# Softmax over two lanes a partition instead of four, and another order of work, in a dynamic convolution with a gated output

## The chip, the core and the metric

The kernel runs on one core of one Trainium2 chip. The metric is the time of the program on the device, in microseconds (us); lower is better. A core has five engines with queues of their own that run in order: TensorE (PE, with its weight loads PEld), VectorE (DVE), ScalarE (ACT), GpSimd (POOL) and SyncE (SP). SP only issues DMAs here, POOL and ACT issue some too. Engines meet through semaphores.

## What is computed

`x` is (8 lanes, 4224 positions, 192 channels), `weight_gen` is (8, 4224, 8 heads, 7 taps). First each position and head gets a softmax over its 7 taps, and the channels of a head (24 each) are convolved causally with these weights:

```
w = softmax(weight_gen, axis=-1)                 # max, subtract, exp, sum, divide
y[b,s,h,:] = sum_k w[b,s,h,k] * x_pad[b, s+k, h, :]
gate = sigmoid(sum_k conv_w[k] * y_pad[:, s+k, :])   # 5 taps, one weight a channel
out  = (gate * (y @ w_val)) @ w_out
```

All of it is in float32.

## The kernel before, in words

**Tiling.** The 4224 positions are cut into 36 groups: 88 positions, then 34 of 120, then 56. Groups go through the engines in pairs (`Pair`): pair 0 is the first group alone, pairs 1 to 17 have two groups, pair 18 is the last alone. A *stage* q is the stretch in which PE does the first step of pair q, the value product of pair q-1 and the output product of pair q-2.

**First step, a matmul with a band.** For a group, `xt` holds 126 positions of `x` on partitions. `tb` holds a band matrix: row i has, for each lane and head, the softmax weights at the places of the outputs that position i feeds. `bank` (L333) multiplies them into PSUM (256 small matmuls a pair), `evac` (L348) copies PSUM to `ringA`, `ringB` and `S` on ACT, `move` (L356, L358) fills holes in the rings by DMAs from POOL.

**How the band is made.** `Softmax` treats a *part* of about 500 positions at a time: `load` (weights of `weight_gen` into `wt`), `max`, `sub`, `exp`, `sum`, `recip`, `norm`, then `halo` (a DMA that copies the first 6 rows of the next block behind each partition's rows), `spread` (four copies on ACT that put the weights into `zt`, with zeros between them) and `store` (DMA of `zt` into `z` in DRAM). `clear_z` writes the zeros of `z` that no store covers. `load_t` (L307) then reads `z` with a pitch that is one half cell short of a row, so that row i lands shifted by i: that is the band. It takes 9 DMAs a group. Ten parts (`parts`, called s0, s1, s2 and p3 to p9 here) use two `z` in turn, and two `wt`.

**In `before`** a partition of `wt` holds 8 positions (`RM`) of four lanes (`LH`); even partitions hold lanes 0 to 3, odd ones lanes 4 to 7, so that `load` and `store` are two DMAs each.

**The rest.** `tap0` (ACT) and `tap` (DVE, L378) do the 5-tap convolution, `sigm` (ACT, L383) the sigmoid, `wvm_`, `wva_`, `wvd_`, `wvb_` (PE, L402 to L415) the value product, `gv` (DVE, L422, L425) multiplies both, `omA`, `omB` (PE, L433, L442) do the output product, `oev` (ACT, L448) evacuates it to `ot`, `store` of `Pair` (SP, L456) writes it out. The four output products of a pair use the PSUM banks ps3, ps3, ps1, ps2, so the second waits until `oev` of the first has emptied ps3.

**What sets the order.** Every step is put in a list by `at(time, step)`, or `st(offset, step)` from the stage's nominal time `when(q)`; at the end the list is sorted by time and issued. The times only order the instructions of each engine's queue: nothing on the chip waits for them. A part first used in pair q (q = 4, 6, ... 16 for p3 to p9) has its steps placed relative to stages q-4 to q-2. A stage with a `spread` in it is called a *spread stage* below (in `before`, stages 4, 6, ... 14, and stage 3 for p3); the stage after it is a *plain stage*.

**The weights** `w_val` and `w_out` arrive as 64-bit patterns and are converted by `convert_weights` (L133 to L144, 8 steps each for three column ranges), then placed by `place_weights` on ACT.

Of the kernel before, what the change touches and what calls it, by code (L numbers as in the profile page):

```python
# [16 lines left out]
def tile_dynconv_gated_moe(  # L17
# [23 lines left out]
    L = B  # L41
# [11 lines left out]
    W = LH * H  # L53
    CELL = 2 * W + 4
# [9 lines left out]
    RM = 8  # L64
# [102 lines left out]
    ROWS = HD * RM  # L167
    zb = [dpool.tile([(1 + 2 * ROWS) * PITCH], FP32, name=f"z{i}") for i in range(2)]

    def clear_z(i, lo, hi, eng):  # L170

        t, n = zb[i], (hi - lo) // P
        for u in range(2):
            dst = bass.AP(tensor=t.tensor, offset=t.offset + (1 + ROWS * u + lo) * PITCH,
                          ap=[[n * PITCH, P], [PITCH, n], [1, PITCH]])
            src = bass.AP(tensor=zero.tensor, offset=zero.offset, ap=[[zero.ap[0][0], P], [0, n], [1, PITCH]])
            eng.dma_start(out=dst, in_=src)
        if lo == 0:
            eng.dma_start(out=t[0:PITCH].rearrange("(p c) -> p c", p=14),
                          in_=zero[0:14, 0:PITCH // 14])  # L180

    class Softmax:


# [59 lines left out]
        def spread(self, e, o):
            R, n = self.R, self.n
            m = NPR - o
            w0, z0 = self.wt[:, 0, e + o, 0:1], zt[:, e, 0:1]
            to = HC2 * (1 - e) + ((e, 1) if e == 0 else (1, CELL))[o]
            src = bass.AP(tensor=w0.tensor, offset=w0.offset + K - 1 - o,
                          ap=[[w0.ap[0][0], self.np], [2 * ROW, R // 2], [2 * (ROW - 1), m], [n * ROW, LH], [K, H]])  # L250
            dst = bass.AP(tensor=z0.tensor, offset=z0.offset + to,
                          ap=[[z0.ap[0][0], self.np], [2 * DATA, R // 2], [CELL, m], [2 * H, LH], [2, H]])
            nc.scalar.copy(out=dst, in_=src)  # L253

        def store(self, engs):
            t, R = zb[self.zi], self.R
            for u in range(2):
                z = zt[u:u + 1]
                src = bass.AP(tensor=z.tensor, offset=z.offset, ap=[[2 * z.ap[0][0], self.np // 2], [DATA, R], [1, DATA]])
                dst = bass.AP(tensor=t.tensor, offset=t.offset + (1 + ROWS * u) * PITCH,  # L260
                              ap=[[R * PITCH, self.np // 2], [PITCH, R], [1, DATA]])
                engs[u % len(engs)].dma_start(out=dst, in_=src)

    class Group:
# [29 lines left out]
        def load_t(self, p, w, lo, hi, eng):  # L294
# [5 lines left out]
            off = (1 + self.s - PAD + lo - p.r0) * PITCH + HC2 + skip * CELL - HC2 * i0  # L300
            src = bass.AP(tensor=b.tensor, offset=b.offset + off,
                          ap=[[PITCH - HC2, hi - lo], [ROWS * PITCH, 2], [1, cells * CELL]])
# [3 lines left out]
                          ap=[[NW * d.ap[0][0], hi - lo], [CELLS * CELL, 2], [1, cells * CELL]])  # L306
            eng.dma_start(out=dst, in_=src)  # L307

    class Pair:
# [12 lines left out]
        def bank(self, gi, kind, b):  # L322
# [357 lines left out]
```

## Time and profile before

| | |
|---|---|
| median of 3 runs | 611.3 us (610.46 to 615.15) |
| the profiled execution | 613.28 us, span 611.5 us |
| mean granted TensorE clock | 0.888 |
| PE busy | 465.6 us (76%) |
| DVE busy | 408.8 us (67%) |
| ACT busy | 310.1 us (51%) |
| POOL busy | 309.9 us (51%) |
| DMA moved | 116.5 MB, mean 191 GB/s |

The span is what the profile covers of the 613.28 us. The chain that ended last is 34% PE, 19% DMA, 15% SP's queue, 13% "issue" (the engine waited for nothing that the profile shows), 8% POOL and 6% DVE. An engine's idle time counts only where another engine, or the end, waits for it.

### The profile page before, as it was taken

Reading aid. Unit: us, or ns where it says so; the run is one execution under the profiler, and the core shown is the slowest. Engines: PE = TensorE matmul, PEld = TensorE weight load, DVE = VectorE, ACT = ScalarE, POOL = GpSimd, SP = SyncE. Lnnn points to the kernel's source line nnn. Section 1 sums busy time; section 2 is a strip of 40 time slices with the busy share of each in tenths; the row PEclk is TensorE's granted clock in tenths of the full one; section 3 lists DMA queues with packets and bytes.
Section 4 is the critical chain, followed back from the end, with each engine's and each line's share of the span. In section 5 each row is a group of like instructions: output and inputs, shape, how many; then the busy total and the mean of one; then the engine's idle time right before and its main releaser. Section 6 shows DMA issues by size and latency. Waiting matters only on the chain.

```text
span 611.5 us, 15672 instructions
## 1 busy us (share of the span) xinstructions
PE 465.6 (76%) x6450; PEld 352.0 (58%) x6450; DVE 408.8 (67%) x311; ACT 310.1 (51%) x427; POOL 309.9 (51%) x532
## 2 busy tenths in 40 slices
PE   5030164768875998699968977996899599899996
PEld 3030153555754776468556846683767396686765
DVE  6708607479872979397849885796679584665950
ACT  5014165436634763675367537655564545545442
POOL 8362627554546184537634581647184709337400
PEclk9556587797988999799979997998899789999999
DMA  8775567573769676967794778678866957563334
GB/s 229 241 190 183 151 205 212 137 241 85 211 181 250 211 199 184 260 181 223 165 308 131 241 186 257 163 218 193 277 158 204 246 155 193 156 197 82 98 98 119
DMA packets 77005, 116.50 MB, mean 191 GB/s; under 512 B 20149, under 2 KB 58624, under 8 KB 76934
## 3 DMA queue, kind: packets, MB, share of 16 engines
q1 hardware_dynamic: 54650, 80.36, 44.3%
q0 software_dynamic: 21296, 34.46, 22.4%
q8 instruction: 51, 0.84, 0.6%
q10 hardware_dynamic: 988, 0.68, 0.4%
q14 instruction: 20, 0.16, 0.1%
HBM read 59.35 MB, written 43.53 MB: 168 GB/s over the span
## 4 chain that ended last, share of the span: by engine, by line
PE 34%; DMA 19%; SPq 15%; issue 13%; POOL 8%; DVE 6%; ACT 4%; POOLq 0%; ACTq 0%; DVEq 0%
SPq L307 12%; PE ps L333 11%; PE ps L433 8%; DMA wt<-in_weight_gen_dram 5%; PE ps L442 5%; PE ps L407 4%; DMA z<-zt 4%; POOL xt L276 3%; POOL ringA L356 3%; DVE aA L378 3%; DMA xt<-in_x_dram 3%; DMA wt<-wt 2%; PE ps L402 2%; PE ps L410 2%; PE ps L415 2%
## 5 line engine op out<-in xcount | busy, mean ns | idle before, releaser
L333 PE MATMUL ps<-tb,xt 126*32 126x120 f32 (+2 forms) x4608 | 142.2, 282 | 98.0 <-DMA tb<-z 40.1
L333 PEld LDWEIGHTS ps<-tb,xt 126*32 126x32 f32 x4608 | 132.6, 115 | 108.1 <-issue 78.9
L276 POOL DMA_DIRECT2D xt<-in_x_dram x264 | 157.2, 623 | 25.8 <-DMA ringA<-S 7.0
L378 DVE SCALAR_TENSOR_TENSOR aA<-ringA,wf,aA 128x1920 f32<-128x1920 f32 (+2 forms) x76 | 157.3, 2070 | 7.8 <-ACT aA L374 3.4
L358 POOL DMA_DIRECT2D ringB<-S x76 | 42.2, 560 | 223.4 <-ACT ringB L348 184.4
L433 PE MATMUL ps<-wf,aA 128*120 128x192 f32 (+2 forms) x576 | 110.5, 348 | 0.0
L433 PEld LDWEIGHTS ps<-wf,aA 128*120 128x120 f32 (+2 forms) x576 | 102.0, 200 | 13.6 <-issue 13.2
L422 DVE TENSOR_TENSOR aA<-ps,aA 128x960 f32<-128x960 f32 (+2 forms) x36 | 39.3, 1130 | 101.3 <-ACT ot L448 57.1
L448 ACT COPY ot<-ps 120x768 f32<-120x768 f32 (+2 forms) x72 | 55.7, 798 | 85.0 <-PE ps L442 53.1
L442 PE MATMUL ps<-wf,aB 64*120 64x192 f32 (+2 forms) x576 | 65.0, 356 | 37.6 <-ACT ot L448 37.6
L378 DVE SCALAR_TENSOR_TENSOR aB<-ringB,wf,aB 128x960 f32<-128x960 f32 (+2 forms) x76 | 86.9, 1144 | 2.0
L356 POOL DMA_DIRECT2D ringA<-S x152 | 81.8, 545 | 7.0 <-issue 4.2
L442 PEld LDWEIGHTS ps<-wf,aB 64*120 64x120 f32 (+2 forms) x576 | 48.7, 193 | 56.7 <-ACT ot L448 46.4
L407 PE MATMUL ps<-ringA,wva 128*128 128x480 f32 (+2 forms) x144 | 63.0, 581 | 3.5 <-ACT ringB L348 3.5
L253 ACT COPY zt<-wt 128x512 f32<-128x512 f32 (+5 forms) x40 | 34.2, 924 | 54.1 <-DMA wt<-wt 33.0
L208 DVE TENSOR_REDUCE mx<-wt 128x256 f32<-128x1792 f32 (+2 forms) x10 | 18.3, 1826 | 49.1 <-DMA wt<-in_weight_gen_dram 49.1
L348 ACT COPY ringA<-ps 128x480 f32<-128x480 f32 (+2 forms) x72 | 36.2, 556 | 27.3 <-PE ps L333 27.3
L407 PEld LDWEIGHTS ps<-ringA,wva 128*128 128x128 f32 x144 | 26.3, 193 | 40.0 <-issue 22.5
L374 ACT ACTIVATE aA<-ringA,wf 128x960 f32<-128x960 f32 (+2 forms) x38 | 37.5, 1031 | 14.5 <-DMA ringA<-S 14.5
L348 ACT COPY S<-ps 128x480 f32<-128x480 f32 (+2 forms) x36 | 19.9, 552 | 46.2 <-PE ps L333 46.1
L383 ACT ACTIVATE aA<-aA 128x1920 f32<-128x1920 f32 (+2 forms) x19 | 32.1, 1690 | 14.3 <-DVE aA L378 14.2
L425 DVE TENSOR_TENSOR aB<-ps,aB 128x480 f32<-128x480 f32 (+2 forms) x36 | 21.5, 637 | 20.8 <-ACT aB L383 20.8
(59 smaller groups left out, 383.0 us busy)
## 6 DMA issues: line engine op xcount, KB each, us to landing
xt<-in_x_dram POOLq DMA_DIRECT2D x264, 94.5 KB, 4.0
out_dram<-ot SPq DMA_DIRECT2D x68, 360.0 KB
tb<-z SPq DMA_DIRECT2D x239, 74.4 KB
z<-zt SPq DMA_DIRECT2D x16, 612.0 KB
wt<-in_weight_gen_dram SPq DMA_DIRECT2D x16, 448.0 KB
wt<-wt SPq DMA_DIRECT2D x9, 588.0 KB
z<-zero SPq DMA_DIRECT2D x4, 1071.0 KB
ringA<-S POOLq DMA_DIRECT2D x136, 30.0 KB, 2.8
```

The costliest lines, as they stand in the source:

```text
L276: eng.dma_start(out=self.xb[0:G * NW, j, 0:D], in_=src)
L307: eng.dma_start(out=dst, in_=src)
L333: nc.tensor.matmul(out=pa[Q * c:Q * c + Q, n * l:n * l + n], lhsT=g.xb[0:k, LH * u + l, C * h:C * h + Q], rhs=t[:, u, PAD // 2:(PAD + n) / ...
L348: nc.scalar.copy(out=dst, in_=pa)
L356: nc.gpsimd.dma_start(out=ringA[q:q + h, LH * u:LH * u + LH, p0:p0 + n], in_=St[p:p + h, :, 0:n])
L358: nc.gpsimd.dma_start(out=ringB[HD * u + q:HD * u + q + h, :, p0:p0 + n], in_=St[p:p + h, :, 0:n])
L378: nc.vector.scalar_tensor_tensor(out=a, in0=self.src(g, j), scalar=cw[:, g, j:j + 1], in1=a, op0=ALU.mult, op1=ALU.add)
L407: nc.tensor.matmul(out=self.v01(e)[:, u], lhsT=wva, rhs=self.A(e, u), start=True, stop=False)
L422: nc.vector.tensor_tensor(out=a, in0=self.v01(e), in1=a, op=ALU.mult)
L433: nc.tensor.matmul(out=ps[b][0:n, u, D * t:D * t + D], lhsT=g[:, u, t], rhs=woa, start=first and t == 0, stop=not first, skip_group_check= ...
L442: nc.tensor.matmul(out=ps[b][0:n, u, D * t:D * t + D], lhsT=g[hs, t], rhs=wob[hs], start=first and t == 0, stop=not first, skip_group_chec ...
L448: nc.scalar.copy(out=ots[0:n, 2 * e + k], in_=ps[b][0:n, :, 0:2 * D])
```

## The change

A partition of `wt` now holds 16 positions of two lanes (`LQ`), and partition 4b+u holds block b of lanes 2u and 2u+1. A cell of the band is half as wide, `tb` has four lane groups instead of two, and `load`, `store` and `clear_z` are four DMAs each. The bytes of `load` and `store` for a part are the same; the halo copies 6 rows of two lanes instead of four. The first part stores whole rows of `z`, zeros included, so nothing has to be cleared for it. Loads, `exp`, `halo`, the taps' sigmoids and much of the first 60 us have other places.

```
-    W = LH * H
-    CELL = 2 * W + 4
+    LQ = 2
+    NL = L // LQ
+    NBL = P // NL
+    W = LQ * H
+    CELL = 2 * W + 2
...
-    RM = 8
+    RM = 16
...
+            self.row = PITCH if i == 0 else DATA
+            self.z = zt[:, 0:R * self.row].rearrange("p (r c) -> p r c", r=R)
...
-                d, n = 2 * (c // R + 1), min(R, PAD - c)
+                d, n = NL * (c // R + 1), min(R, PAD - c)
...
-            for u in range(2):
-                z = zt[u:u + 1]
-                src = bass.AP(tensor=z.tensor, offset=z.offset, ap=[[2 * z.ap[0][0], self.np // 2], [DATA, R], [1, DATA]])
...
+            for u in range(NL):
+                z = self.z[u:u + 1]
+                src = bass.AP(tensor=z.tensor, offset=z.offset, ap=[[NL * z.ap[0][0], p], [self.row, R], [1, self.row]])
...
-                          ap=[[PITCH - HC2, hi - lo], [ROWS * PITCH, 2], [1, cells * CELL]])
+                          ap=[[PITCH - HC2, hi - lo], [ROWS * PITCH, NL], [1, cells * CELL]])
...
-                        rhs=t[:, u, PAD // 2:(PAD + n) // 2, l, h, :],
+                        rhs=t[:, (LH * u + l) // LQ, PAD // 2:(PAD + n) // 2, l % LQ, h, :],
...
-    at(7.1, s0.halo, (nc.sync, nc.scalar, nc.sync))
+    at(7.5, s0.halo, (A, A))
...
-    at(8.5, s1.exp)
+    at(11.55, s1.exp)
...
-            at(when(a) + (8.0 if q > 4 else 2.0), p.load, u, nc.sync)
+            at(when(q - 5) + 12.5 if q > 5 else when(1) + (1.0 if q < 5 else 12.0), p.load, u, SP)
...
+        at(t1 + 1.5 if q <= 4 else when(q - 3) + 7.5, p.exp)
...
-        at(when(a + 2) + 4.0, p.halo, (nc.sync,))
+        at(when(q - 2) + 3.3, p.halo, (SP,))
...
-            at(when(a + 2) + 8.0 + 0.9 * i, p.spread, i // 2, i % 2)
+            at(when(q - 2) + 8.0 + 0.01 * i, p.spread, i // 2, i % 2)
...
-            st(6.5, p1.sigm, 0)
-            st(11.0, p1.sigm, 1)
+            st(11.5 if q > 1 else 6.1, p1.sigm, 0)
+            st(16.4 if q > 1 else 6.5, p1.sigm, 1)
```

The tables of times move the following. In the rows a line number is that of the program, a name with a number is one buffer, "x4" means four in a row.

ACT in a spread stage and the end of it, before (L348 `evac`, L383 `sigm`, L253 `spread`, L363 the rings' halo, L448 `oev`, L374 `tap0`):

```order
L348 COPY ringA<-ps_92 128x4x120 x2
L383 ACTIVATE aA_76<-aA_76 128x1920
L253 COPY zt<-wt_65 128x4x4x32
L253 COPY zt<-wt_65 128x4x3x32
L253 COPY zt<-wt_65 128x4x4x32
L253 COPY zt<-wt_65 128x4x3x32
L383 ACTIVATE aB_79<-aB_79 128x960
L363 COPY ringA<-ringA 128x8x4
L363 COPY ringB<-ringB 128x4x4
L448 COPY ot<-ps_94 120x768
L374 ACTIVATE aA_77<-ringA,wf 128x960 x2
L448 COPY ot<-ps_94 120x768
```

and in the changed kernel:

```order
L354 COPY ringA<-ps_92 128x4x120 x2
L257 COPY zt<-wt_65 128x8x4x16
L257 COPY zt<-wt_65 128x8x3x16
L257 COPY zt<-wt_65 128x8x4x16
L257 COPY zt<-wt_65 128x8x3x16
L389 ACTIVATE aA_76<-aA_76 128x1920
L369 COPY ringA<-ringA 128x8x4
L369 COPY ringB<-ringB 128x4x4
L454 COPY ot<-ps_94 120x768
L380 ACTIVATE aA_77<-ringA,wf 128x960
L389 ACTIVATE aB_79<-aB_79 128x960
L380 ACTIVATE aA_77<-ringA,wf 128x960
```

The first `oev` stands ahead of the second sigmoid, which stood ahead of it, and the `spread` ahead of the first. The `exp` of the next part, which followed in before at the end of this stage (L216, with a table load), has gone to the plain stage, behind the evacuations there.

SP in a spread stage, before (L307 `load_t`, L234 `halo`, L199 `load`, L262 `store` of z, L456 output):

```order
L456 DMA out_dram<-ot 120x2x384 x4
L307 DMA tb_63<-z_97 14x2x476
L307 DMA tb_63<-z_97 14x2x680 x7
L307 DMA tb_63<-z_97 14x2x476
L234 DMA wt_66<-wt_66 112x4x336
L234 DMA wt_66<-wt_66 14x4x336
L307 DMA tb_64<-z_97 14x2x476
L307 DMA tb_64<-z_97 14x2x680 x7
L307 DMA tb_64<-z_97 14x2x476
L199 DMA wt_65<-in_weight_gen_dram 64x4x448 x2
L262 DMA z_98<-zt 512x1x306 x2
L456 DMA out_dram<-ot 120x2x384 x4
```

and in the changed kernel:

```order
L202 DMA wt_65<-in_weight_gen_dram 32x2x896 x4
L462 DMA out_dram<-ot 120x2x384 x4
L237 DMA wt_66<-wt_66 112x2x336
L237 DMA wt_66<-wt_66 12x2x336
L313 DMA tb_63<-z_97 14x4x238
L313 DMA tb_63<-z_97 14x4x340 x7
L313 DMA tb_63<-z_97 14x4x238
L313 DMA tb_64<-z_97 14x4x238
L313 DMA tb_64<-z_97 14x4x340 x7
L313 DMA tb_64<-z_97 14x4x238
L268 DMA z_98<-zt 512x1x153 x4
L462 DMA out_dram<-ot 120x2x384 x4
```

The halo has moved ahead of the first group's nine `tb` loads, and the load of `weight_gen` into the stage before, behind its `tb` loads.

DVE around the first taps and the first gate product (L422, L425), before:

```order
L242 TENSOR_TENSOR wt_65<-wt_65,mx_67 128x4x448
L378 SCALAR_TENSOR_TENSOR aA_76<-ringA,wf,aA_76 128x704 x3
L378 SCALAR_TENSOR_TENSOR aB_79<-ringB,wf,aB_79 128x352
L378 SCALAR_TENSOR_TENSOR aA_76<-ringA,wf,aA_76 128x704
L378 SCALAR_TENSOR_TENSOR aB_79<-ringB,wf,aB_79 128x352 x3
L422 TENSOR_TENSOR aA_76<-ps_91,aA_76 128x704
L425 TENSOR_TENSOR aB_79<-ps_93,aB_79 128x352
L208 TENSOR_REDUCE mx_68<-wt_66 128x256
```

and in the changed kernel (L147 is the last conversion step, which reads what POOL has computed; L211 to L245 are the softmax of part p3):

```order
L147 SCALAR_TENSOR_TENSOR wf<-ot,wf 128x2x192 x2
L384 SCALAR_TENSOR_TENSOR aA_76<-ringA,wf,aA_76 128x704 x4
L384 SCALAR_TENSOR_TENSOR aB_79<-ringB,wf,aB_79 128x352 x4
L211 TENSOR_REDUCE mx_68<-wt_66 128x256
L215 TENSOR_TENSOR wt_66<-wt_66,mx_68 128x2x896
L223 TENSOR_REDUCE mx_68<-wt_66 128x256
L227 TENSOR_SCALAR mx_68<-mx_68 128x256
L228 RECIPROCAL mx_68<-mx_68 128x256
L245 TENSOR_TENSOR wt_66<-wt_66,mx_68 128x2x896
L428 TENSOR_TENSOR aA_76<-ps_91,aA_76 128x704
L431 TENSOR_TENSOR aB_79<-ps_93,aB_79 128x352
```

The whole softmax of p3 now stands ahead of the first gate product, and four of eight conversion steps of each weight run on POOL. On PE the order of the matmuls is the same in both kernels.

## Rows read from the trace of the kernel before

**Rows 1.** Page, part 2: PE's busy tenths in 40 slices of the span.

```profile
PE   5030164768875998699968977996899599899996
```

**Rows 2.** Busy time by stage: stretch, length, engines (instructions), PE clock, DMA share, GB/s.

```profile
73.70:99.40 25.70, 14.81 (x278) 10.97 (x279) 5.93 (x6) 11.51 (x19) 8.17 (x15) 0.77 0.63 183
...
128.30:165.40 37.10, 26.38 (x360) 19.90 (x360) 33.33 (x25) 22.49 (x28) 19.07 (x34) 0.86 0.59 171
165.40:203.30 37.90, 28.22 (x356) 21.84 (x356) 20.38 (x14) 16.38 (x22) 16.04 (x28) 0.86 0.83 230
...
403.80:435.50 31.70, 26.74 (x358) 20.57 (x356) 21.68 (x16) 17.47 (x24) 16.06 (x28) 0.89 0.80 229
435.50:462.20 26.70, 24.25 (x362) 18.58 (x363) 22.33 (x16) 16.52 (x22) 16.03 (x28) 1.00 0.67 190
...
496.40:520.40 24.00, 24.00 (x362) 18.54 (x361) 13.12 (x11) 12.96 (x20) 16.04 (x28) 1.00 0.63 173
...
546.70:570.40 23.70, 23.70 (x358) 18.18 (x356) 16.87 (x13) 13.05 (x20) 10.78 (x18) 1.00 0.44 115
```

**Rows 3.** Timeline of ACT in stage 12: start, length, operation, [idle before, releaser].

```profile
421.07 3.74 ACT L253 COPY zt<-wt 128x512 f32<-128x512 f32 x4 [3.90 <-DMA tb<-z]
...
425.83 0.78 ACT L448 COPY ot<-ps 120x768 f32<-120x768 f32 x1
...
437.45 1.70 ACT L216 ACTIVATE wt<-wt 128x1792 f32<-128x1792 f32 x1 [2.83 <-DVE wt L212]
```

**Rows 4.** Timeline of PE in stages 12 and 13.

```profile
426.67 1.64 PE L442 MATMUL ps<-wf,aB 64*120 64x192 f32 x8 [4.96 <-ACT ot L448]
428.24 5.84 PE L433 MATMUL ps<-wf,aA 128*120 128x192 f32 x24
...
439.89 5.53 PE L333 MATMUL ps<-tb,xt 126*32 126x120 f32 x190 [2.45 <-ACT ot L448]
...
456.56 4.17 PE L433 MATMUL ps<-wf,aA 128*120 128x192 f32 x24
```

**Rows 5.** Timeline of DVE in stage 12.

```profile
404.35 2.03 DVE L242 TENSOR_TENSOR wt<-wt,mx 128x1792 f32<-128x1792 f32 x1
...
433.34 2.02 DVE L208 TENSOR_REDUCE mx<-wt 128x256 f32<-128x1792 f32 x1 [6.37 <-DMA wt<-in_weight_gen_dram]
```

**Rows 6.** Timeline of SP's DMA issues in stage 12.

```profile
407.55 7.76 SPq L307 DMA_DIRECT2D tb<-z  x9
415.42 1.54 SPq L234 DMA_DIRECT2D wt<-wt  x2
...
424.84 1.40 SPq L199 DMA_DIRECT2D wt<-in_weight_gen_dram  x2
```

**Rows 7.** Timeline of all engines in the first 75 us.

```profile
16.66 3.69 POOL L487 MEMSET tb<- 128x4284 f32 x1
...
17.54 2.22 SPq L234 DMA_DIRECT2D wt<-wt  x2
...
28.96 1.24 ACT L253 COPY zt<-wt 112x128 f32<-112x128 f32 x4 [14.32 <-DMA wt<-wt]
...
37.32 2.75 SPq L199 DMA_DIRECT2D wt<-in_weight_gen_dram  x2
...
40.42 4.92 PE L333 MATMUL ps<-tb,xt 126*32 126x88 f32 x128 [30.39 <-DMA xt<-in_x_dram]
...
47.87 2.02 DVE L208 TENSOR_REDUCE mx<-wt 128x256 f32<-128x1792 f32 x1 [20.88 <-DMA wt<-in_weight_gen_dram]
...
57.34 1.73 SPq L262 DMA_DIRECT2D z<-zt  x2
...
73.71 5.03 PE L333 MATMUL ps<-tb,xt 126*32 126x120 f32 x128 [28.37 <-DMA tb<-z]
```

**Rows 8.** One line's instructions, for L307 and for L262: ns min/median/max.

```profile
L307 SPq DMA_DIRECT2D tb<-z x320: 676/789/1938, 33.3 to 554.6; - x160
...
L262 SPq DMA_DIRECT2D z<-zt x19: 564/634/1302, 30.2 to 485.7; - x19
```

More of the change, by code (lines that the diff above doesn't have):

```diff
@@ new lines, in tile_dynconv_gated_moe @@
+    at(0.5, lambda: clear(tb[1], 0, 0, cs, A))
+    at(0.6, lambda: clear(tb[1], 1, 0, cs, A))
+    at(0.7, lambda: clear(tb[1], 2, 0, cs, V))
+    at(0.8, lambda: clear(tb[1], 3, 0, cs, G_))
+    at(0.9, lambda: G_.memset(xt[0][:, :, :], 0.0))
+    for i in (1, 2):
+        at(0.95, lambda i=i: G_.memset(xt[i][:, :, D:XC], 0.0))
+    at(4.1, s0.max)
+    at(4.7, s0.sub)
+    at(5.3, s0.exp)
+    at(6.0, s0.sum)
+    at(6.6, s0.recip)
+    at(7.4, s0.norm)
+    at(7.5, s0.halo, (A, A))
+    at(8.0, gr[0].load_x, G_)
@@ L552, in tile_dynconv_gated_moe @@
-    at(17.7, s2.exp)
-    at(24.0, s2.sum)
-    at(24.1, s2.recip)
-    at(24.2, s2.norm)
-    at(24.3, s2.halo, (nc.sync,))
-    for i in range(4):
-        at(31.0 + 0.1 * i, s2.spread, i // 2, i % 2)
-    at(32.0, s2.store, (nc.sync,))
-    at(33.0, clear_z, 1, 3 * P, 4 * P, nc.sync)
-    s0.ready, s1.ready, s2.ready = 11.4, 20.0, 32.0
-    def jobs(p, q):
-        a = max(q - 4, 1)
-        for u in range(2):
-            at(when(a) + (8.0 if q > 4 else 2.0), p.load, u, nc.sync)
-        for i, f in enumerate((p.max, p.sub, p.exp)):
-            at(when(a) + 20.6 + 0.1 * i, f)
+    at(11.5, s0.store, (A, SP))
@@ new lines, in tile_dynconv_gated_moe @@
+    at(17.0, s1.halo, (SP,))
+    at(17.1, lambda: clear(tb[0], 3, 0, CELLS, V))
+    for u in range(NL):
+        at(17.2, s2.load, u, SP)
+    for i in range(4):
+        at(20.0 + 0.1 * i, s1.spread, i // 2, i % 2, (A, A, G_, A)[i])
+    at(20.9, s1.store, (SP,))
+    at(21.0, lambda: G_.memset(wts[1][96:P], 0.0))
+    for k in range(2):
+        at(21.1 + 0.1 * k, lambda k=k: clear(tb[1], 2 * k, cs, CELLS, G_))
+        at(21.1 + 0.1 * k, lambda k=k: clear(tb[1], 2 * k + 1, cs, CELLS, G_))
@@ new lines, in tile_dynconv_gated_moe @@
+    for i, f in enumerate(place_weights()):
+        at(30.0 + 0.35 * i, f)
+    at(20.0, s2.max)
+    at(20.1, s2.sub)
+    at(20.2, s2.exp)
+    at(26.0, s2.sum)
+    at(26.1, s2.recip)
+    at(26.2, s2.norm)
+    at(29.2, clear_z, 0, 112, 80, 5, SP)
+    at(29.3, s2.halo, (SP,))
+    for i in range(4):
+        at(34.0 + 0.1 * i, s2.spread, i // 2, i % 2)
+    at(35.0, s2.store, (SP,))
+    at(46.0, clear_z, 1, 336, 16, 11, SP)
+    s0.ready, s1.ready, s2.ready = 11.5, 20.9, 35.0
+    for p in parts[3:]:
+        q = next(q.q for q in pairs if p.use < q.s + q.n)
+        for u in range(NL):
+            at(when(q - 5) + 12.5 if q > 5 else when(1) + (1.0 if q < 5 else 12.0), p.load, u, SP)
+        t1, t2 = when(q - 4) + 20.6, when(q - 3) + 20.6
+        if q <= 4:
+            t1, t2 = when(1) + 9.0, when(1) + 12.5
+        for i, f in enumerate((p.max, p.sub)):
+            at(t1 + 0.1 * i, f)
+        at(t1 + 1.5 if q <= 4 else when(q - 3) + 7.5, p.exp)
```

191 lines of the change are left out of this document (86 added, 105 removed).

## The prediction

> **What bounds the kernel now.** I read the page's slices first. PE is nearly full over the last two thirds and nearly idle over the first ten slices of 15.3 us [rows 1]. So there are two places to look: the start, and what keeps the middle from being full.
>
> The view by stage splits the middle. From 165.4 to 546.7 us stand 13 stages of the same matmuls. [...] So the floor of a stage is about 23.8 us, and 381.3 us for 13 stages is 72 us above 13 x 23.8 = 309.
>
> The timelines of stage 12 show where those microseconds go. ACT stands 3.90 us before the spread, waiting for a DMA; the name given is a `tb` load, but the halo was issued at 415.42, behind nine `tb` loads on SP, ended its issue at 416.96, and the spread starts 4.1 us later [rows 3, 6]. Spread (3.74 us) and second sigmoid stand ahead of `oev`, which starts at 425.83. PE waits 4.96 us for it, since the next output product needs its bank [rows 3, 4]. Behind the wait the same 24 matmuls take 5.84 us instead of the 4.17 us of the next stage: the granted clock is 0.89 over the stage and 1.00 over the next [rows 2, 4]. At the end of the stage `weight_gen` was issued only at 424.84, DVE stands 6.37 us for it, ACT's `exp` then waits 2.83 us for DVE's subtraction, and the two `oev` behind the exp hold PE for another 2.45 us [rows 3 to 6].
>
> **Part 1: the 13 stages.** PE's matmuls are unchanged in kind, number and order. In a spread stage the change takes away three things.
> - The halo goes ahead of the nine `tb` loads (7.76 us [rows 6]). It needs `norm`, which ended at 406.38, 2.6 us after the stage began [rows 2, 5]. So it is issued by about +4.2 us and, with the same 4.1 us to the spread, there at about +8.3, when ACT comes out of its evacuations. ACT's 3.90 us go. On SP the `tb` loads start 0.4 us later at most: they waited for PE until 407.55 anyway.
> - The first `oev` waits for PE alone. Spread from +8.5 to +12.3, the first sigmoid after the taps, then `oev` at about +16.3 (the second sigmoid and two small copies take 1.0 us between 424.81 and 425.83 [rows 3], the first, on twice the elements, 2 us); PE needs it at +17.9 (426.67 less the 4.96 us wait). The 4.96 us go, and with them the slow clock (5.84 - 4.17 = 1.67 us in these 24 matmuls alone).
> - The load is issued a stage earlier, the exp stands in the plain stage behind the evacuations, 20 us after its subtraction. DVE's 6.37, ACT's 2.83 and PE's 2.45 us go.
>
> What is late next? DVE: 21.68 + 22.33 = 44.0 us of work in two stages [rows 2], against 47.6 us at the floor. In the spread stage sum to norm, 9 taps' worth and the wait for PE fill it; about 0.5 us is spare. Moving the sigmoids costs nothing while that holds: the second one now runs between the first and second `tap0`, and its product follows it at once.
>
> What is added: two more issues for each load and store. A store issue is 634 ns, a `tb` issue 789 ns [rows 8]; 4 x 0.7 = 2.8 us in two stages. SP's issues of two stages are 36 `tb` (28 us) and about 11 us of others, so it has room: nothing on the path. Packets are half as long in `tb` and `z`, the halo's bytes are half.
>
> The DMA share was 0.80 and 0.67 in these two stages [rows 2]; the same work in 49 us is (31.7 x 0.80 + 26.7 x 0.67) / 49 = 0.88. So landings get longer than in the stages at the floor (0.63, 0.44), and I do not take the floor itself. Between 23.8 and the plain stage's 26.7 I take **24.6 us**, nearest to the plain stage less its wait, 26.7 - 2.45 = 24.25, and a little more for the DMAs. 13 x 24.6 = 320 against 381.3: **-61 us**; ends: 23.8 (-72) and 26.0 (-43).
>
> **Part 2: the start.** (a) First group: the halo of s0 was issued at 17.54, behind x loads and zeros on SP, and its spread began at 28.96 [rows 7]. Now ACT issues it right behind norm. Norm ends about 9.3 (0.9 us later than now, since ACT issues two more DMAs and the load is four), the halo takes the 4 to 5 us seen above: spread at 14. From spread to PE's first band matmul took 40.42 - 28.96 = 11.5 us. The store is now 640 KB instead of 268, at 180 GB/s 2 us more [rows 2]. First matmul at about 27.5, 13 us earlier.
> (b) Second part: s1's exp now waits behind s0's band loads on ACT, so its norm ends at 29 (14 + 1.2 spread + 5 store and landing + 2.5 three issues + 1.3 exp + 5 sum to norm), its halo and then the load of s2 are issued at 30. From that load's first issue to s2's maximum took 10.5 us (37.32 to 47.87 [rows 7]); maximum, subtraction, exp and the last spread of s1, which stands behind that exp, take 6.6 us. Store of s1 at 47 instead of 57.34; to PE's stage 1 then 16.4 us as before [rows 7]. Stage 1 starts at **63 instead of 73.7**.
> (c) Conversion: GpSimd has arithmetic of its own nowhere in this trace. The nearest row for its eight elementwise steps is its memset, 3.69 us for 4284 elements [rows 7], 0.33 us for 384. I take 1 us a step, more than the memset since operands are read too; ends 0.3 and 3 us. The second conversion's last step stands on POOL behind stage 1's hole moves, so its sum is hidden unless the eight take over 12 us. [...]
> (d) From there the first gate product is the chain, since p3's softmax, 10 us, stands ahead of it on DVE. Stage 1's hole moves end near 75 and the conversion at 76, the first pair's taps at 82; p3's load, behind 4 x 400 rows of zeros (2.3 MB) on SP, is there by 85; its softmax ends at 96. Stage 2 starts at 98, against 99.4: nearly nothing left. But then SP is ahead. Stage 3 at 121.5 and stage 4 at **148 instead of 165.4**, since stages 2 and 3 lose the waits for `tb` and exp that make the third 37.1 us [rows 2]. **-17 us**, ends -4 and -27.
>
> **Part 3: the end** from 546.7 on is unchanged: 64.8 us.
>
> Sum: 148 + 320 + 64.8 = 532.8 us of span. The profiled execution took 613.28 us for a span of 611.5, so 534.6; the median of the runs is 2 us under it, so **533 us**.
>
> **The rivals.**
> *A wait stays in the spread stage.* If DVE's norm comes late, SP holds 18 `tb` loads behind the halo, and the spread reaches into `oev` again. For it: 0.5 us spare on DVE and a DMA share of 0.88. Against: PE ran a stage of 24.0 us with the DMAs at 0.63 [rows 2]. Price: 4 to 5 us of PE and 1.7 us of clock, 6 us in each of six spread stages: 36, so 569 us. [...]
> *PE's floor is reached.* 13 x 23.8 and a start 4 us better: 518 us.
> *The start fails alone*: gain of the stages only, 611 - 61 = 550 us; I count it with the first rival.
> *Slower: SP becomes the bound.* Each `tb` load has 56 rows instead of 28. If issue time went with rows, 789 ns becomes 1.58 us: 36 x 1.58 + 11 = 68 us, and 6 us of waits for `oev`, 74 in two stages against 58.4. Six and a half times 15.6 is 101 us: 611 - 17 + 101 = 695 us. It decides from a `tb` issue of about 1.15 us ((58.4 - 17) / 36). Against: a store of z has 512 rows and takes 634 ns [rows 8].
> *The change does not do what it says*: the order of the instructions shows each move; what it cannot show is the halo's landing.
>
> **Numbers.** Forecast (523 to 545) 0.47; better (under 523) 0.15; a wait stays or the start fails (545 to 590) 0.28; between 590 and 605, 0.02; no change 0.02; slower 0.06. A measurement of this kernel can tell 1% (6 us) from no change. Faster by over 1%: 0.92. Range for 8 in 10: 514 to 575, leaving out the best of the better cases and the worst of the partial ones.
>
> **What would show it.** Right: in the stages from 4 on no wait of PE for `oev`, granted clock 1.00 in the spread stages too, stage lengths of 24 to 25 us that do not alternate; no wait of DVE for `weight_gen`; first band matmul at 27 to 28 us, stage 1 near 63. Wrong: ACT idle ahead of the spread; SP issuing `tb` at over 1 us; DVE idle ahead of the second conversion's last step; DMA share over 0.95 with PE waiting for `xt` or `tb`.

## The result, and the profile after

The changed kernel takes 575.82 us (median of 4 runs, 575.13 to 579.41) against 612.52 us (4 runs): a ratio of 0.941, 95% interval 0.935 to 0.947. It is 37 us faster; the forecast was 533 us, 78 faster, in a range up to 575. So the direction was right and the gain less than half of what was forecast. Runs more than 1.5% slower than the fastest run of their kernel are left out of medians and ratios, here and below. The profiled execution took 576.01 us for a span of 574.2.

Page of the changed kernel, part 2, 40 slices of 14.4 us (before: [rows 1]):

```profile
PE   5030081382899999989898999899899999999986
PEclk9565577596899999999999999999999999999999
```

From the eleventh slice on, 144 us, PE is full and its clock high: the middle is mended. In the first ten it stands still even more than before. The stages, by the view of busy time (columns as in [rows 2]; stages 12, 13 and 17, then the 13 stages from 4 to 16 as one stretch):

```profile
383.94:409.02 25.08, 24.52 (x359) 18.97 (x357) 23.05 (x16) 16.71 (x24) 15.86 (x28) 1.00 0.73 210
409.02:435.03 26.01, 24.55 (x358) 18.90 (x356) 20.83 (x16) 17.34 (x23) 15.84 (x28) 1.00 0.84 229
...
509.28:533.41 24.13, 24.13 (x358) 18.55 (x356) 16.96 (x13) 12.98 (x20) 10.77 (x18) 1.00 0.46 120
...
174.63:509.28 334.65, 318.95 (x4631) 244.07 (x4629) 275.93 (x190) 213.25 (x287) 202.07 (x358) 1.00 0.80 225
```

The 13 stages take 334.65 us instead of 381.3: -46.6, where -61 was forecast. Spread and plain stages are now of one length, 25.08 and 26.01 in the row pair that was 31.70 and 26.70. Stage 4, though, starts at 174.63 and not at 165.4: the part ahead of it lost 9 us where a gain of 17 was forecast. The tail, 64.9 us, is as it was. So 26.6 of the 41 us that were missed lie ahead of stage 4, 14.6 in the 13 stages.

**The middle.** ACT's and SP's timelines in stage 12 of the changed kernel (before: [rows 3, 6]):

```profile
393.38 3.83 ACT L257 COPY zt<-wt 128x512 f32<-128x512 f32 x4
397.08 1.83 ACT L389 ACTIVATE aA<-aA 128x1920 f32<-128x1920 f32 x1
...
401.28 0.80 ACT L454 COPY ot<-ps 120x768 f32<-120x768 f32 x1 [2.16 <-PE ps L448]
```

```profile
386.64 2.69 SPq L237 DMA_DIRECT2D wt<-wt  x2
389.43 15.91 SPq L313 DMA_DIRECT2D tb<-z  x18
```

The halo goes out 2.7 us into the stage and the spread begins without any wait where the evacuations end. At the evacuation of the output ACT now waits 2.16 us for PE, where PE waited 4.96 us for ACT [rows 4]. What is left of PE's waits in the 13 stages (waits of PE: on whom, us in total, times, longest):

```profile
PE ps L339 <- issue: 14.2, 12, 2.8
PE ps L408 <- issue: 1.5, 1, 1.5
```

Before, the same stretch had, among others, these:

```profile
PE ps L442 <- ACT ot L448: 35.5, 6, 6.5
PE ps L333 <- ACT ot L448: 7.8, 5, 2.5
...
PE ps L333 <- issue: 4.3, 5, 1.7
```

So 35.5 us of waits for the first evacuation and 7.8 us for the last ones went, and 11.4 us more of a wait that no engine releases came (15.7 instead of 4.3). In 12 of 13 cases it lies inside the band matmuls, once just behind them, some 24 matmuls further on from stage to stage. PE's timeline of the changed kernel, stages 4 to 6:

```profile
174.63 6.70 PE L339 MATMUL ps<-tb,xt 126*32 126x120 f32 x225
182.66 1.01 PE L339 MATMUL ps<-tb,xt 126*32 126x120 f32 x28 [1.32 <-issue]
...
200.36 7.33 PE L339 MATMUL ps<-tb,xt 126*32 126x120 f32 x248
208.60 0.43 PE L339 MATMUL ps<-tb,xt 126*32 126x120 f32 x8 [0.91 <-issue]
...
225.62 4.33 PE L339 MATMUL ps<-tb,xt 126*32 126x120 f32 x144
231.31 3.44 PE L339 MATMUL ps<-tb,xt 126*32 126x120 f32 x112 [1.36 <-issue]
```

A stage has 256 band matmuls and 100 others, each with a weight load. From the first wait to the second are 31 + 100 + 248 = 379 pairs, 758 instructions; from the second to the third 8 + 100 + 144 = 252 pairs, 504. That is 3 times 253 and twice 252. The page of the changed kernel, parts 1 and 3, has PE's instructions (the rows of PE and PEld) and a queue of transfers of instructions (packets, MB, share):

```profile
PE 453.5 (79%) x6450; PEld 345.3 (60%) x6450; DVE 400.8 (70%) x304; ACT 311.8 (54%) x428; POOL 320.6 (56%) x552
...
q8 instruction: 51, 0.84, 0.6%
```

12,900 instructions in 51 transfers are 253 a transfer. So the waits seem to stand where one piece of PE's program ends and the next is not there yet; the profile does not say whose instructions the queue carries, so this is inferred from the spacing, and the name *waits for instructions* below rests on that. Whether they depend on what else the DMA engines carry is asked below.

**The start.** Timelines of the changed kernel by engine: PE's first band matmuls of stages 0 to 3, then ACT, SP and DVE:

```profile
34.66 4.73 PE L339 MATMUL ps<-tb,xt 126*32 126x88 f32 x128 [24.91 <-DMA tb<-z]
71.62 5.95 PE L339 MATMUL ps<-tb,xt 126*32 126x120 f32 x128 [32.23 <-DMA tb<-z]
...
110.08 5.57 PE L339 MATMUL ps<-tb,xt 126*32 126x120 f32 x128 [21.40 <-DVE aA L428]
...
148.57 6.06 PE L339 MATMUL ps<-tb,xt 126*32 126x120 f32 x201
```

```profile
10.45 3.17 ACTq L237 DMA_DIRECT2D wt<-wt  x2
...
23.06 1.26 ACT L257 COPY zt<-wt 112x128 f32<-112x128 f32 x4 [7.42 <-DMA wt<-wt]
...
136.79 3.68 ACT L257 COPY zt<-wt 128x512 f32<-128x512 f32 x4 [13.66 <-DMA tb<-z]
```

```profile
6.23 4.17 SPq L180 DMA_DIRECT2D z<-zero  x4
...
62.99 14.64 SPq L313 DMA_DIRECT2D tb<-z  x17
77.68 5.41 SPq L180 DMA_DIRECT2D z<-zero  x4
83.19 4.16 SPq L237 DMA_DIRECT2D wt<-wt  x2
...
118.83 6.26 SPq L180 DMA_DIRECT2D z<-zero  x4
125.21 6.55 SPq L237 DMA_DIRECT2D wt<-wt  x2
```

```profile
59.51 2.02 DVE L245 TENSOR_TENSOR wt<-wt,mx 128x1792 f32<-128x1792 f32 x1
...
95.14 2.02 DVE L211 TENSOR_REDUCE mx<-wt 128x256 f32<-128x1792 f32 x1 [8.16 <-DMA wt<-in_weight_gen_dram]
...
107.20 2.02 DVE L245 TENSOR_TENSOR wt<-wt,mx 128x1792 f32<-128x1792 f32 x1
...
143.62 2.22 DVE L428 TENSOR_TENSOR aA<-ps,aA 128x960 f32<-128x960 f32 x2 [19.38 <-ACT aA L389]
```

Read in order: the first halo went out at 10.45 and its spread began at 23.06, 12.6 us later; 1.9 MB of zeros had been issued at 6 to 10 us. The norm of s2 ended at 61.5 but its halo was issued at 83.19, behind 17 loads of `tb` (*band loads* below) and four DMAs of zeros; p3's load stood behind that, and DVE waited for it. The norm of p3 ended at 109.2, its halo was issued at 125.21, behind eleven band loads, the load of p4 and zeros, and since the spread now stands ahead of the sigmoid, DVE's gate product waited 19.38 us for ACT and PE's stage 3 for both.

### The profile page after: what moved, and what is told of

Read it like the earlier page. It is cut to its first block, busy times and chain, and to the rows that moved or that the text cites. A ratio compares the mean times of both kernels' runs of the same rounds, so it can differ in the third digit from the quotient of the medians.

```text
span 574.2 us, 15747 instructions
## 1 busy us (share of the span) xinstructions
PE 453.5 (79%) x6450; PEld 345.3 (60%) x6450; DVE 400.8 (70%) x304; ACT 311.8 (54%) x428; POOL 320.6 (56%) x552
## 4 chain that ended last, share of the span: by engine, by line
PE 70%; DMA 11%; issue 6%; SPq 4%; DVE 3%; ACT 3%; POOL 2%; ACTq 1%; DVEq 0%; POOLq 0%
PE ps L339 22%; PE ps L439 16%; PE ps L413 10%; PE ps L448 9%; PE ps L408 5%; PE ps L416 5%; PE ps L421 4%; DMA ringA<-S 2%; DMA wt<-in_weight_gen_dram 2%; DMA wt<-wt 2%; SPq L313 2%; POOL xt L282 1%; DMA z<-zt 1%; DVE aA L384 1%; DMA ringB<-S 1%
## 5 line engine op out<-in xcount | busy, mean ns | idle before, releaser
L339 PE MATMUL ps<-tb,xt 126*32 126x120 f32 (+2 forms) x4608 | 145.4, 285 | 99.3 <-DMA tb<-z 59.7
L339 PEld LDWEIGHTS ps<-tb,xt 126*32 126x32 f32 x4608 | 136.1, 114 | 108.3 <-issue 84.9
L282 POOL DMA_DIRECT2D xt<-in_x_dram x272 | 159.2, 619 | 12.8 <-DMA ringA<-S 5.9
L439 PE MATMUL ps<-wf,aA 128*120 128x192 f32 (+2 forms) x576 | 102.9, 332 | 0.0
L439 PEld LDWEIGHTS ps<-wf,aA 128*120 128x120 f32 (+2 forms) x576 | 93.9, 188 | 12.9 <-issue 12.1
L448 PE MATMUL ps<-wf,aB 64*120 64x192 f32 (+2 forms) x576 | 60.6, 338 | 13.6 <-ACT ot L454 13.6
L448 PEld LDWEIGHTS ps<-wf,aB 64*120 64x120 f32 (+2 forms) x576 | 46.6, 184 | 30.2 <-ACT ot L454 18.4
L413 PE MATMUL ps<-ringA,wva 128*128 128x480 f32 (+2 forms) x144 | 61.8, 571 | 0.0
L257 ACT COPY zt<-wt 128x512 f32<-128x512 f32 (+5 forms) x39 | 33.7, 937 | 35.5 <-DMA tb<-z 13.7
L413 PEld LDWEIGHTS ps<-ringA,wva 128*128 128x128 f32 x144 | 25.8, 189 | 36.2 <-issue 23.5
L380 ACT ACTIVATE aA<-ringA,wf 128x960 f32<-128x960 f32 (+2 forms) x38 | 39.2, 1034 | 2.7 <-DMA ringA<-S 2.7
L408 PE MATMUL ps<-ringA,wvm 128*32 128x480 f32 (+2 forms) x288 | 35.1, 557 | 2.4 <-issue 1.5
L389 ACT ACTIVATE aA<-aA 128x1920 f32<-128x1920 f32 (+2 forms) x19 | 32.2, 1693 | 2.9 <-DVE aA L384 2.8
```

The lines of the kernel that those rows point to most:

```text
L282: eng.dma_start(out=self.xb[0:G * NW, j, 0:D], in_=src)
L339: nc.tensor.matmul(out=pa[Q * c:Q * c + Q, n * l:n * l + n], lhsT=g.xb[0:k, LH * u + l, C * h:C * h + Q], rhs=t[:, (LH * u + l) // LQ, PAD ...
L408: nc.tensor.matmul(out=self.v2(e)[c:c + Q], lhsT=wvm[:, Q * i:Q * i + Q], rhs=self.A(e, u), start=True, stop=False, tile_position=(0, c))
L413: nc.tensor.matmul(out=self.v01(e)[:, u], lhsT=wva, rhs=self.A(e, u), start=True, stop=False)
L439: nc.tensor.matmul(out=ps[b][0:n, u, D * t:D * t + D], lhsT=g[:, u, t], rhs=woa, start=first and t == 0, stop=not first, skip_group_check= ...
L448: nc.tensor.matmul(out=ps[b][0:n, u, D * t:D * t + D], lhsT=g[hs, t], rhs=wob[hs], start=first and t == 0, stop=not first, skip_group_chec ...
```

## The experiments

Times are medians; the ratio is to the kernel before, on the same chip, with its 95% interval. Stage starts are of one profiled execution each; kernels with the same start as the changed one had stage 0 at 31.4 to 34.7 us, stage 1 at 67.2 to 71.6 and stage 4 at 166.7 to 176.4, so differences of that size tell nothing alone.

**Zeros later.** Edit: `at(0.3, clear_z, 1, 0, 112, 3, SP)` becomes `at(17.4, ...)`, behind the load of s2.

> Edit: the 1.9 MB of zeros for the second z, which SP issued at 6 to 10 us, are issued behind the load of s2. Theory (the first halo took 11.8 us to land because these zeros stood ahead of it in the DMA queue): halo lands 4 to 5 us after its issue, first band matmul at 27 to 28.5 us instead of 34.66, stage 1 near 64.5 instead of 71.62, whole time 568 to 571 us. Rival (the halo is slow by itself, or POOL's reordering of the weights holds it up): first band matmul at 33 us or later, whole time 574 to 578 us.

566.82 us, ratio 0.928 (0.925 to 0.931): below the interval of the changed kernel. ACT and PE of this kernel:

```profile
10.23 1.39 ACTq L237 DMA_DIRECT2D wt<-wt  x2
...
14.98 1.26 ACT L257 COPY zt<-wt 112x128 f32<-112x128 f32 x4 [1.34 <-DMA wt<-wt]
```

```profile
26.57 4.61 PE L339 MATMUL ps<-tb,xt 126*32 126x88 f32 x128 [15.89 <-DMA tb<-z]
63.15 6.02 PE L339 MATMUL ps<-tb,xt 126*32 126x120 f32 x128 [31.97 <-DMA tb<-z]
```

The spread begins 4.75 us after the halo's issue, the first band matmul at 26.57, stage 1 at 63.15, both below what the kernels with the zeros early had. The theory holds. Stages 2, 3 and 4 came at 102.81, 141.50 and 166.69.

**The halos and p3's load ahead, three kernels with a slip.** Edit on SP: the halo of s2 and the load of p3 to 20.9005 and 20.9007, the halo of p3 to 41.6, ahead of the zeros (the load of p4, at 41.5, stays ahead of it, other than the texts below say); the second kernel has the zeros later too, the third also `wts[1]`'s memset ahead of p3's load.

> Edit: on SP the halo of s2 and the load of p3 go ahead of the 17 band loads of stage 1, and the halo of p3 ahead of the load of p4 and of the zeros. Theory (stages 2 and 3 start late because these short issues stood behind long ones on SP, 22 us and 16 us after their norm; ACT's spread waits for the halo, and sigmoid, evacuations and exp stand behind the spread): stage 2 at 96 to 100 instead of 110.08, stage 3 at 120 to 126 instead of 148.57, whole time 546 to 554 us. Rival (DVE, ACT and POOL have too much to do there whatever SP's order): stage 2 not before 106, stage 3 not before 140, whole time over 565 us.

> Edit: both of the edits before. If both theories hold and the gains add: first band matmul 27 to 28.5, stage 1 near 64.5, stage 2 near 91, stage 3 near 115, whole time 539 to 547 us. If the zeros, moved, now stand in the way of the load of s2 or of the store of s1: stage 1 not before 70, whole time as with the second edit alone.

> Edit: as the two edits together, but POOL's memset of the partitions from 96 on in the second wt stands ahead of the load of p3 again (in the kernels with the second edit it stood behind it, waited for the load with all of POOL behind it, and wiped the weights of p3 on these partitions). Theory (short issues behind long ones on SP make stages 2 and 3 late): stage 1 near 63, stage 2 at 88 to 94, stage 3 at 113 to 119, whole time 538 to 547 us. Rival (DVE, ACT, POOL or the sum of SP's issues bound these stages whatever the order): stage 2 not before 99, whole time over 555 us.

570.94 us, 564.01 and 563.42, ratios 0.933 (0.928 to 0.937), 0.926 (0.920 to 0.931), 0.922 (0.917 to 0.927). The times in the list also set the order of the program, and these put each of the two halos ahead of its own norm: the copied rows are not divided, and norm waits for the halo. Stage 1 came at 64.0 in the third, but stage 2 at 113.6. They show nothing on SP's order.

**The same without the slip.** Edit: `s2.sum`, `recip`, `norm` at 20.75 to 20.77, DVE's first conversion steps from 20.3 on, `s2.halo` at 20.9005 and p3's load at 20.9007 on SP, p3's halo at 41.8, zeros later. Here too p4's load, at 41.5, stays ahead of p3's halo.

> Edit: the three kernels with the halo of s2 and p3 moved on SP had it ahead of its norm in the program too, so that norm waited for the halo and the copied rows were not divided. Here norm is moved ahead of it on DVE (behind the exp of s2, 2 us of conversions ahead of it), the zeros of the second z stand behind the load of s2, the halo of s2 and the load of p3 ahead of the band loads of stage 1, the halo of p3 ahead of the load of p4 and the zeros. Theory (short issues behind long ones on SP make stages 2 and 3 late): stage 1 at 63 to 67, stage 2 at 89 to 96, stage 3 at 114 to 121, whole time 539 to 549 us. Rival (DVE, ACT, POOL or the sum of SP's issues bound these stages whatever the order): stage 2 not before 99, whole time over 555 us.

562.62 us, ratio 0.921 (0.913 to 0.929). Stage 1 at 66.79, stage 2 at 100.64, stage 3 at 131.68, stage 4 at 159.31 (of a profiled execution of 567.79 us). Against the zeros later alone that is 2 us at stage 2 and 10 at stage 3. DVE's gate product waits 10.98 us for ACT, where it stood 19.38, but stage 2 missed the forecast and the whole time met the rival's bound. Stage 2 now waits for its band loads: p3's softmax ended at 94.97, but the store of s2's band, at 85.73, stood behind seven band loads on SP. And p3's halo went out at 108.08, still 13 us behind its norm. So SP's order was a part of it; whether it was all, this kernel does not decide, since its order on SP was mended only in part.

**A start worked out again, and its mended form.** Edit: zeros for s1 at 17.4 as above, halo of s2 and load of p3 on ACT, `s2.spread` at 28.0, its store at 28.5, p3's maximum at 29.6 and exp at 33.0; then the zeros for s2 at 17.45 (first kernel) or at 20.9003, behind the store of s1 (second; p3's sum at 36.0, its halo at 39.0, the last zeros at 40.0).

> Edit: a start worked out from the waits seen: all zeros that s1 and s2 need behind the load of s2, halo of s2 and load of p3 on ACT, which stands idle there, the spread of s2 ahead of ACT's evacuations of stage 1, its store ahead of the last zeros, maximum of p3 between the two conversions on DVE and its sum behind the first gate product. Theory: stage 1 at 63 to 65, stage 2 at 87 to 91, stage 3 at 111 to 117, whole time 534 to 543 us. Rival (4.1 MB of zeros now stand ahead of the store of s1 and of the band loads): stage 1 at 68 or later, whole time over 545 us.

> Edit: the start of the kernel before it, but the zeros that s2 needs stand behind the store of s1, the last zeros behind the band loads of stage 2, and the sum of p3 ahead of the first gate product. Theory (the zeros ahead of the store of s1 cost stage 1 its 9 us, the last zeros ahead of the band loads stage 2 its 7): stage 1 at 63 to 67, stage 2 at 87 to 92, stage 3 at 111 to 117, whole time 541 to 550 us. Rival (2.2 MB of zeros now delay the band loads of stage 1 as much): stage 1 at 69 or later, whole time 553 to 560 us.

559.55 us, ratio 0.916 (0.911 to 0.921), and 557.59, ratio 0.912 (0.908 to 0.915). The first had stages 1 to 4 at 72.77, 104.91, 127.19 and 155.19. The second, by SP and PE:

```profile
51.06 11.31 SPq L180 DMA_DIRECT2D z<-zero  x4
```

```profile
74.00 5.93 PE L339 MATMUL ps<-tb,xt 126*32 126x120 f32 x128 [42.66 <-DMA tb<-z]
...
97.31 6.19 PE L339 MATMUL ps<-tb,xt 126*32 126x120 f32 x128 [8.32 <-DMA tb<-z]
```

In both the rival on stage 1 held: it came at 72.77 and 74.00 against 63.15 with these zeros behind the band loads. In the second SP needs 11.31 us to issue four of them; the band loads went out at 62.48 instead of 54.45. Still stage 2 comes at 97.31 and stage 4 at 154.50, 20 us ahead of the changed kernel's 174.63.

**The order alone.** Edit: the kernel before, with the new times from stage 4 on only:

```
-            at(when(a) + (8.0 if q > 4 else 2.0), p.load, u, nc.sync)
+            at(when(q - 5) + 12.5 if q > 4 else when(a) + 2.0, p.load, u, nc.sync)
...
+        at(when(a + 1) + 7.5 if q > 4 else when(a) + 20.8, p.exp)
...
-        at(when(a + 2) + 4.0, p.halo, (nc.sync,))
+        at(when(a + 2) + (3.3 if q > 4 else 4.0), p.halo, (nc.sync,))
...
-            at(when(a + 2) + 8.0 + 0.9 * i, p.spread, i // 2, i % 2)
+            at(when(a + 2) + 8.0 + (0.01 if q > 4 else 0.9) * i, p.spread, i // 2, i % 2)
...
```

Taps and sigmoids have the places of the change.

> Edit: the kernel before, four lanes a partition and its start as they were, with the new places of load, exp, halo, spread, taps and sigmoids from stage 4 on. Theory (the order of the steps takes the waits away, the narrow cell only makes band matmuls 0.38 us a stage slower and adds packets that hold up PE's own instruction fetch): stage 4 at 165, 13 stages of 24.0 to 24.6 us, whole time 543 to 552 us. Rival (it takes the layout, whose halo is half as large): ACT still waits for the halo in the spread stages, these take over 27 us, whole time over 560 us.

582.23 us, ratio 0.952 (0.948 to 0.957): neither. Its 13 stages took 344.8 us, 36.5 of the 46.6 us that the whole change takes off them. ACT stood 8.50 us ahead of the spread in stage 4, the first of the new order, 32.2 us long, and 1 to 2 us three times later; the other stages took 24.3 to 29.0 us, and PE waited for the first evacuation of the output once, in stage 4. What kept it from the forecast is mostly PE's wait for instructions:

```profile
PE ps L333 <- issue: 19.9, 13, 3.3
```

So most of the gain of the middle is the order's; no run has the layout without the order. Without stage 4 its stages average 26.05 us ((511.98 - 199.34) / 12), those of the changed kernel 25.74. The waits for instructions are not due to the narrower layout's packets, since the old layout has them too.

**One step of the order undone at a time**, in the changed kernel. Halo: `when(q - 2) + 3.3` becomes `+ 4.0` from p4 on.

> Edit: the changed kernel with the halo of the parts from p4 on back behind the first nine band loads of its stage. Theory (the place of the halo is what takes ACT's wait ahead of the spread away): the halo lands 7 to 8 us later, PE waits 4 to 6 us for the first evacuation of the output in each of the six spread stages, whole time 598 to 612 us. Rival (the halo, now of half the bytes, would land in time anyway): no wait, whole time 574 to 580 us.

606.41 us, ratio 0.992 (0.988 to 0.995). ACT's spread and SP's halo in stage 10, and PE's waits in the 13 stages:

```profile
357.81 3.69 ACT L257 COPY zt<-wt 128x512 f32<-128x512 f32 x4 [7.72 <-issue]
```

```profile
351.84 1.54 SPq L237 DMA_DIRECT2D wt<-wt  x2
```

```profile
PE ps L448 <- ACT ot L454: 22.0, 6, 5.0
```

The halo goes out 11.6 us into the stage (340.22). The profile names no releaser of ACT's 7.72 us; the spread starts 4.4 us after the halo's issue ended. Six waits for the evacuation, 22 us, are back and the 13 stages take 367.0 us. The theory holds.

Load and exp: `when(q - 5) + 12.5` becomes `when(q - 4) + 8.0`, exp right behind the subtraction.

> Edit: the changed kernel with the load of the parts from p4 on a stage later and the exp right behind the subtraction, as before the change. Theory (DVE waits for the load, ACT's exp for DVE, the last evacuations of the output behind the exp hold PE for about 2.5 us in every second stage): whole time 588 to 596 us, with DVE waits for weight_gen of 4 us and more. Rival (once the halo is early SP issues the load early enough): whole time 574 to 580 us.

617.87 us, ratio 1.011 (1.001 to 1.021): 42 us lost where 12 to 20 were expected. Load and exp were put back together, so their shares are not told apart. DVE and PE at the beginning of stage 11:

```profile
385.77 2.02 DVE L211 TENSOR_REDUCE mx<-wt 128x256 f32<-128x1792 f32 x1 [7.80 <-DMA wt<-in_weight_gen_dram]
```

```profile
392.32 7.24 PE L339 MATMUL ps<-tb,xt 126*32 126x120 f32 x192 [8.79 <-ACT ot L454]
```

The mechanism is the one forecast, its price is not: with the other waits gone PE reaches the end of the stage earlier (24.3 us behind its start, against 31.7 in stage 12 of before), while the exp comes hardly earlier (32.7 us behind it against 33.7), and stands 8.8 to 9.1 us there, five times, not 2.45 [rows 4].

Sigmoids and taps: offsets 6.5, 11.0, -2.5 and 6.0 as before, from stage 4 on.

> Edit: the changed kernel with both sigmoids, from stage 4 on, ahead of the first evacuation of the output and the first one ahead of the spread again, as before the change. Theory (with the halo early there is room: 16.3 us become 17.3, PE needs the evacuation 17.9 us into the stage): no wait, whole time 573 to 579 us. Rival (the order on ACT is what took the wait away): PE waits 1 to 5 us for the evacuation in each of six spread stages, whole time 582 to 606 us.

572.48 us, ratio 0.938 (0.930 to 0.947): the same as the changed kernel. One wait for the evacuation, of 0.4 us, in 13 stages. Once the halo is early, their place costs nothing.

**What PE's wait for instructions depends on.** Outputs of stages 4 to 15 not stored:

> Edit: the changed kernel without the stores of the outputs in stages 4 to 15, so those outputs are left out. Theory (PE waits inside the band matmuls for its own instructions, whose transfers stand in the full DMA engines at the start of each stage): with 1.4 MB a stage less there these waits fall from 15.9 us to under 4 us, stages of 24.2 to 24.5 us, whole time 562 to 567 us. Rival (the fetch is slow whatever else the DMAs do, or the wait is something else): waits of 14 to 17 us, whole time 573 to 578 us.

559.74 us, ratio 0.917 (0.911 to 0.922). PE's waits in the 13 stages:

```profile
PE ps L339 <- issue: 7.1, 7, 2.2
```

From 15.7 to 7.1, at a DMA share of 0.65 instead of 0.80, and the 13 stages take 325.0 us instead of 334.65 (in a profiled execution of 565.07 us). The time came out under the forecast, the waits above it. More than half went, not three quarters. That is clear of chance: in eight kernels whose stages 4 to 16 are those of the changed one, these waits sum to 13.6 to 17.5 us. So they depend on what the DMA engines carry; what holds the other half is not shown.

Three of four stores of a stage put to 31.0, behind the next pair's first nine band loads:

> Edit: the changed kernel with three of the four output stores of a stage issued 8 us later, between the band loads of the next pair's two groups. Theory (the same): the waits of PE for its instructions are at least halved, whole time 564 to 571 us. Rival (other transfers fill the DMA engines there anyway): waits as before; SP's band loads of the second group come 2 us later for nothing, whole time 574 to 582 us.

572.76 us, ratio 0.936 (0.930 to 0.942), within the interval of the changed kernel:

```profile
PE ps L339 <- issue: 4.3, 4, 2.7
...
PE ps L408 <- issue: 0.6, 1, 0.6
```

The waits for instructions fell to 4.9 us, but at matmul 128, where the second group begins, PE now stands twice for DMAs, 2.45 us (put down to `z<-zt`) and 2.17 us (`tb<-z`), and the 13 stages take 335.7 us: the gain was given back. The DMA share is 0.81 here, so the mean share does not set these waits. Nor does it elsewhere: at 0.73 the kernel with the halo behind had 13.3 us of them and the one with load and exp back 2.5, in which PE also stood 44.8 us for ACT. So what matters seems to be which transfers run beside the band matmuls.

The same on top of the mended start, and there, by itself, the load of `weight_gen` between the band loads of the two groups (`when(q - 5) + 6.9`):

> Edit: the kernel with the zeros split, and three of four output stores of a stage issued between the band loads of the next pair's groups. Theory (fewer waits of PE for its instructions, as seen with the late stores alone): 3 to 8 us under the kernel with the zeros split. Rival (band loads come late instead): within 2 us of it, or slower.

> Edit: the kernel with the zeros split, and the load of weight_gen for the parts from p4 on issued between the band loads of the two groups of its stage instead of behind both, so that its 0.9 MB land in the middle of a stage and not beside the band matmuls of the next. Theory (what the DMA engines carry beside the band matmuls sets PE's wait for instructions): the waits in the stages behind a load halve, 3 to 6 us under the kernel with the zeros split. Rival (other transfers fill the DMA engines there): within 2 us.

552.66 us, ratio 0.904 (0.898 to 0.909), and 551.57, ratio 0.901 (0.895 to 0.906), against 0.912 (0.908 to 0.915) without either. The first's interval overlaps, and its 13 stages took 334.8 us, as without: inconclusive. In the second, whose interval lies below, the waits for instructions are 9.0 us instead of 13.6 and the 13 stages take 331.2 instead of 334.9, 3.7 of the 6 us. The two are not told apart; they are the fastest kernels of this study, 23 and 24 us under the changed one.

## Why the prediction was wrong, point by point

Two steps failed, both in Part 2: the landing of the first halo, and the claim that stage 2 loses its waits. Part 1 had the mechanism right and one term too small.

- **Part 1, the three waits taken away: right.** The halo, and load and exp together, are each worth over 30 us when put back, and no wait of PE for `oev` or of DVE for `weight_gen` is left. The clock came back as forecast, 1.00 in every stage. The place of the sigmoids, which the second item counts on, cost nothing and gained nothing.
- **Part 1, the size: 24.6 us a stage was 25.74.** The floor of 23.8 was read from stages of the old layout (24.00 and 23.70 us, at a granted clock of 1.00 [rows 2]); the 256 band matmuls, 7.17 us there, take 7.55 in the stage at 509.28, and that stage takes 24.13 us: 0.38 us of matmuls a stage are 5 us in 13 stages. And where 0.8 us were added for longer landings, 1.2 us a stage are waits for instructions, and 0.4 us lie elsewhere. The row for it was in the trace of before (4.3 us in these stages, small beside the waits that went), and the prediction left it out. The DMA share was 0.80, not 0.88.
- **Part 2 (a), "the halo takes the 4 to 5 us seen above: spread at 14": this step failed.** It took 12.6 us behind 1.9 MB of zeros. With the zeros away it takes 4.75 us, the first matmul starts at 26.57 (forecast 27.5) and stage 1 at 63.15, where 63 was forecast; (b) was right once (a) holds: the load of s2 goes out at 31.14 there (30 forecast) and the store of s1 at 47.29 (47). In the changed kernel stage 1 was 8.6 us late.
- **Part 2 (c): right.** Four steps of each conversion run on GpSimd, 0.5 to 1.5 us each (1 us was taken for each of the eight), and stage 2 does not wait for them. DVE did stand 9.80 us ahead of the second conversion's last step, one of the signs of being wrong, but for ACT's placing of the first weight; p3's load, which DVE needs behind the taps, came later still. In the second conversion that last step (80.24) runs ahead of GpSimd's last one (87.25), so it does not read all that GpSimd computes.
- **Part 2 (d), the second step that failed:** "since stages 2 and 3 lose the waits". Stage 3 did (26.06 us, forecast 26.5); stage 2 took 38.49 us instead of 23.5. p3's halo stood behind band loads, a load and zeros on SP and held spread, sigmoid, gate product and PE. Stage 1 took 38.46 us instead of 35: p3's load was "there by 85; its softmax ends at 96" in the forecast and came at 95, mostly since stage 1 was late already, but the softmax took 14 us instead of 11, with DVE waiting 3.79 us for the exp behind spread and sigmoids on ACT. So the 26.6 us ahead of stage 4 are 8.6 from (a), 3.5 from stage 1, 15.0 from stage 2, less 0.4 in stage 3. The step counted each queue's durations but not SP's place of the halos, though it was the very thing that Part 1 rests on. The mended start has stage 2 at 97.31 (forecast 98), but from a stage 1 at 74.00 instead of 63 and with halo and load on ACT, so that this number agrees is luck; stage 4 came at 154.50 and not 148: 6.5 us of the forecast were not found, with PE waiting for band loads.
- **Part 3 and the rivals:** the tail was 64.9 us, as forecast. Of the rivals "the start fails alone" came nearest in mechanism, but its 550 us took the start of before as the worst case; the start became 9 us worse, with the bound put at 4 us better. The 569 us of "a wait stays in the spread stage" is nearer as a number, by luck: no such wait stayed. SP's issues stayed at 0.79 us, so the slower rival fell.

## What to carry to other kernels

When a change moves a short DMA ahead of long ones in the steady part, look for the same DMA in the start, where here the zeros and the band loads stood ahead of it, and list every queue's order there by itself. Look at the stage starts one by one: what is late may only be carried over from the stage before. Undoing one step at a time prices a wait better than the row that it had before, because here the price grew as the other waits went (2.45 us became 8.8 to 9.1). Once an engine runs without waits, look at the waits that nobody releases.

## What was not expected of the hardware

PE waited up to 2.85 us with no engine to release it, each time at a multiple of some 253 of its instructions: 15.7 us in 13 stages, 7.1 us without the stores of the outputs and 4.9 us with three of four stores later. That missing instructions are the cause is inferred from the spacing; that the waits depend on the traffic beside them is shown, but not as a function of the mean DMA share.

The same 256 band matmuls take 7.55 us instead of 7.17 with the narrower cell of `tb`, both in stage 17 at a granted clock of 1.00. The old layout in the new order takes 7.16 (stage 17 of the order alone), so it comes with the layout; why is open.

The first arithmetic that POOL runs on the weights, in the changed kernel (start, length):

```profile
62.87 2.15 POOL L362 DMA_DIRECT2D ringA<-S  x4
65.17 0.51 POOL L140 TENSOR_SCALAR wf<-wf 128x384 f32<-128x384 uint32 x1
```

It starts 0.15 us behind the DMA issue ahead of it and takes 0.51 us, as the same step of the second conversion does at 74.78; the estimate was 1 us a step.
